# Converting 64-bit weight pieces in pairs, with stages at their own steps, in a fused attention and SwiGLU kernel

## The chip, the cores and the metric

The kernel runs on one core of a Trainium2 chip. A core has five engines with a queue of instructions each, which work side by side and wait for each other by semaphores: TensorE (PE) multiplies matrices, VectorE (DVE) and ScalarE (ACT) work element by element, GpSimd (POOL) does so too, and SyncE (SP) starts DMA transfers. Matrix results land in PSUM; all else is kept in SBUF, 128 partitions wide. The metric is the time of one execution on the device in microseconds (us), as the median of several. Each engine carries out its instructions in the order of the program, so an instruction that waits holds up all behind it on its engine.

## The reference

q, k and v have the shape (8 sequences, 12 heads, 448 tokens, 64), in float32. The output of attention is the input of a feed-forward block with 768 model columns and 1536 inner columns, whose weights are float64.

```python
def rmsnorm(x, g):
    rms = np.sqrt(np.mean(x * x, axis=-1, keepdims=True) + 1e-06)
    return x / rms * g
q_n, k_n = (rmsnorm(q, g_q), rmsnorm(k, g_k))
scores = 1.0 / np.sqrt(64) * np.matmul(q_n, k_n.transpose(0, 1, 3, 2))
attn = np.exp(scores - np.max(scores, axis=-1, keepdims=True))
attn = attn / (np.sum(attn, axis=-1, keepdims=True) + 1e-09)
x = np.matmul(attn, v)                    # then (8, 12, 448, 64) -> (3584, 768)
xn = x / np.sqrt(np.mean(x * x, axis=-1, keepdims=True) + 1e-06) * rms_g
g = xn @ w_gate                           # float64 weights
return ((g * (1.0 / (1.0 + np.exp(-g)))) * (xn @ w_val)) @ w_out
```

## The kernel before

**Blocks.** The work of attention is cut into 48 blocks `g`, each of two heads of one sequence; six blocks make a sequence. For each block TensorE turns q and k (`turn`, L544, L548), ScalarE and VectorE move them to SBUF (qT L549; kT L550, L552), TensorE makes the scores (`score` L562, `rests` L659), ScalarE the exponentials `e` (L566, L664), and one block later TensorE multiplies them with v (`values`, L576, L589, L674) and sums them over the keys (`den`, L580, L606, L692). VectorE inverts the sum and weighs the result into `x` (L596 to L598, L638). The norms of q and k are prepared two blocks ahead: ScalarE squares (L493), VectorE adds up (`ms`, L496), GpSimd raises to the power -1/2 (`rs`, L514, L515) and scales q (`qn`, L520); k is scaled by its norm within the exponential in the early blocks, and later by ScalarE beforehand (`norm_k`, L530). The last 64 tokens of the heads (`rest`) have steps of their own, on GpSimd L465, L466 and L469, in some blocks. GpSimd also adds the squares of `x` (`ss`, L644), for the norm of the rows (`rms_x`, L726 to L730; `norm_x`, L738, L744).

**Early and later blocks.** Blocks 0 to 6 have attention alone. From block 7 on the steps of attention stand between matrix products of the feed-forward block for the sequence before (L1440, L1081 and others), which are taken from a list `todo`. There the sums over keys are prepared by adding the six tiles of exponentials of a block into one (`later_sums`, `es`, L709 and L714), so that TensorE has fewer to add.

**The order of work.** It is written out in the program. Every step of TensorE goes through `pe(fn)`, which counts the step in `now["t"]` and then gives out what has fallen due; `after(n, fn)` sets work for n steps later. The order on each engine is that in which the program gives the instructions out.

**The weights.** [...] A weight is read as two 32-bit words, the low one and the high one, and put together to a float32 by integer operations. There are 72 pieces of 128 x 384 weights: 48 of gate and value, 24 of the output. A piece goes through this chain, in `convert`: SP loads both words into `raw` (384 KB); ScalarE makes `top` from the high words (Abs, L842) and scales the low words in place (L843), both at stride two, since the words alternate (`split`); VectorE limits `top`, shifts and masks it, and puts in the sign (`join`, L848, L849, L850); GpSimd adds low and top to the finished piece `w` (L890); SP stores a copy in DRAM (`keep`), because the pieces do not all fit in SBUF and are loaded again for each sequence. One call of `convert` takes one step of the chain for several pieces at once: the sum of piece n-5, the join of n-4, the split of n-3, the load of n, the copy of n-7. Early blocks call it three times each (`turns`, L1641 and L1644); later the list of products calls it before each product whose piece is not ready. `TURNS` is 79. Pieces wait in 7 buffers `raw`, 6 buffers `top` (and some of the pool `xs`), and 23 buffers `w`. When all are done, weights derived from sums and differences of pieces are made on VectorE (L1003) for later sequences, and the room of `raw` and `top` serves as further buffers.

The functions that the change touches, and what calls them, with the line numbers of the profile:

Of the kernel before, what the change touches and what calls it, by code (L numbers as in the profile page):

```python
# [25 lines left out]
BW = 384  # L26
# [309 lines left out]
def safe_scores(  # L336
# [367 lines left out]

    def later_sums(g, n):

        def first():
            st["es", g] = tmp.tile([128, S], F32, name="es", tag="es", bufs=2)
            nc.gpsimd.tensor_tensor(st["es", g], st["e", g, 0], st["e", g, 1], ALU.add)  # L709
            more(2)  # L710

        def more(*parts):
            for i in parts:
                nc.gpsimd.tensor_tensor(st["es", g], st["es", g], st["e", g, i], ALU.add)  # L714

        after(n, first)
        after(n + 2, lambda: more(3, 4))
        after(n + 3, lambda: more(5, 6))
# [97 lines left out]
    def room(n):  # L816
        return len(free_w) >= n
# [5 lines left out]
    def data(key):  # L823
        return st[key][0][:, 0:BW]

    def load_raw(src):
        raw = raw_pool.tile([128, 2 * BW], I32, name="raw")
        a = src.shape[1]
        nc.sync.dma_start(out=raw.rearrange("p (a n w) -> p a (n w)", a=a, w=2).bitcast(I64), in_=src)
        return raw  # L830

    def split(raw, n):


        words = raw.rearrange("p (n w) -> p n w", w=2)
        lo, hi = words[:, :, 0], words[:, :, 1]
        if n < 24 and n % 7 > 3:

            top = s_pool.tile([128, 3, HT], I32, name="xs")[:, 0:2].rearrange("p c n -> p (c n)")[:, 0:BW]
        else:  # L840
            top = cv_pool.tile([128, BW], I32, name="top")
        nc.scalar.activation(top.bitcast(F32), hi.bitcast(F32), ACT.Abs)  # L842
        nc.scalar.activation(lo, lo.bitcast(U32), ACT.Copy, scale=2.0**-29)  # L843
        return lo, hi, top

    def join(lo, hi, top):
# [4 lines left out]
        return lo, top  # L851


    pieces = []
# [10 lines left out]
    turn_of = {"n": 0}  # L865
    room_so = []
    TURNS = len(pieces) + 7

    def home(key):
        if key[0] == "w":  # L870
# [6 lines left out]
    def keep(key):  # L877
        nc.sync.dma_start(out=home(key), in_=data(key))

    def convert():  # L880

        n = turn_of["n"]
        if n >= TURNS or not room(1):
            return False
        turn_of["n"] += 1
        if 0 <= n - 5 < len(pieces):
            key = pieces[n - 5][0]
            st[key] = block()
            lo, top = st.pop(("cv", n - 5))
            nc.gpsimd.tensor_tensor(data(key).bitcast(I32), top, lo, ALU.add)  # L890
        if 0 <= n - 4 < len(pieces):
            st["cv", n - 4] = join(*st.pop(("cv", n - 4)))
        if 0 <= n - 3 < len(pieces):
            st["cv", n - 3] = split(st.pop(("raw", n - 3)), n - 3)
        if n < len(pieces):
            st["raw", n] = load_raw(pieces[n][1])
        if 0 <= n - 7 < len(pieces):
            keep(pieces[n - 7][0])
        if turn_of["n"] == TURNS:

            free_w.extend(cv_pool.tile([128, BW], F32, name="top") for _ in range(4))
            whole = [raw_pool.tile([128, 2 * BW], F32, name="raw") for _ in range(7)]
            room_so.extend(whole[:6])
            homes = [whole[6][:, 0:BW], whole[6][:, BW:]] + [cv_pool.tile([128, BW], F32, name="top")[:, :] for _ in range(2)]
            carried.extend(t.rearrange("p (c n) -> p c n", c=KG) for t in homes)
        return True

# [55 lines left out]

    def ask():

        if turn_of["n"] < TURNS:
            return
        while asked["n"] < len(uses):  # L970
            key = uses[asked["n"]]
# [483 lines left out]
    def gate_value_items(b):  # L1455

        if b == 0:
            return [(3 * S, 4 * (fc + 1) + 7, 0, fn) for fc in range(NFC) for fn in plain(fc)]
        return [(6 * HT, TURNS, 8 * (fp + 1) if b == 1 else 0, fn) for fp in range(NFP) for fn in quad(b, fp)]

    def out_items(b):
        if in_quads(b):
            return [(cost, TURNS, 0, fn) for cost, fn in out_quads(b)]
        if b >= FIRST_O:
            return [(NFP // 2 * HALF, TURNS, 0, fn) for fn in out_strassen(b)]
        tiles = out_pairs(b)[-1][1] + 1
        return [(NFC // OUT_PARTS * HALF, 4 * NFC + NFC * (n + 1) + 7, 0, lambda a=(b, n, i, part, i == tiles - 1): project_out(*a))
                for n in range(2) for i in range(tiles) for part in range(OUT_PARTS)]


# [3 lines left out]
    def fill(n=None):  # L1474
# [6 lines left out]
                part["spent"] += todo[n][0]  # L1481
                n += 1
        for _ in range(min(n, len(todo))):
            _, turns, sums_made, fn = todo.pop(0)
# [115 lines left out]
    for g in range(NG + 1):  # L1600
# [7 lines left out]
        if g == 0:  # L1608
# [6 lines left out]
            squares(2, 0)  # L1615
            squares(2, 1)
            pe(lambda: turn(1, 1))
            for _ in range(3):
                convert()
            load_pair(3)  # L1620
            load_v(2)
            convert()
            load_rows()
            continue
        if g <= NPAIR:
# [115 lines left out]
```

## Time and profile before

| what | us |
|---|---|
| median of 3 runs | 1545.07 (1543.91 to 1545.62) |
| the profiled execution | 1546.19 |
| its span, first to last instruction | 1544.4 |
| TensorE busy | 1511.2 (98%) |
| VectorE busy | 929.8 (60%) |
| GpSimd busy | 736.4 (48%) |
| ScalarE busy | 534.8 (35%) |
| mean granted TensorE clock | 0.996 |

The span is a little shorter than the time of the execution that it comes from. In the profile an instruction is named by engine, line, operation and tile (`w<-top,raw` reads top and raw and writes w), with its partitions x elements; `[2.93 <-ACT e L664]` behind it means that its engine stood idle 2.93 us before it, until the instruction on L664 of ScalarE had ended. In a row of waits stand the total, the count and the longest. In a row of windows stand, after the length, the busy time of PE, of its weight loads, of DVE, ACT and POOL with their instruction counts, then the granted clock, the share of the DMA engines and GB/s. Busy shares of the whole span mix stages: conversion fills the first 260 us, and the rest of the span has none of it.

### The profile page before, as it was taken

To read this page: it belongs to the slowest core of one execution; us is meant where nothing else is said; L and a number is where in the kernel's file an instruction comes from. 1 tells how busy PE (TensorE), PEld (TensorE's weight loads), DVE (VectorE), ACT (ScalarE), POOL (GpSimd) and SP (SyncE) were. 2 spreads that over 40 slices of the span, in tenths; PEclk is the share of its full clock that TensorE was granted. 3 is DMA by queue.
4 is the path that set the end of the run, shared out by engine and by line. 5 is a ranking of instruction groups with operands and counts; after the bars stand their busy time and mean duration, and the time that the engine had idled before them with its cause. 6 is when DMAs were issued, how large, how long until landed. Compare 5 with 4: busy or idle time off the path is not lost.

```text
span 1544.4 us, 26111 instructions
## 1 busy us (share of the span) xinstructions
PE 1511.2 (98%) x8900; PEld 1187.4 (77%) x8900; DVE 929.8 (60%) x1793; ACT 534.8 (35%) x1241; POOL 736.4 (48%) x718
## 2 busy tenths in 40 slices
PE   8999998999999999999999999999999999999997
PEld 4344444688856888888987888767987889899997
DVE  5788998667754666854457443444458444673464
ACT  6856664333323333234233332424333232101000
POOL 6868887546424354474435652544545731030003
PEclk9999999999999999999999999999999999999998
DMA  7758575776989978886557855584557755577565
GB/s 194 228 153 258 175 228 157 225 229 214 294 274 275 310 253 266 285 250 188 160 163 217 267 176 153 152 275 131 174 155 228 240 160 148 164 256 256 175 194 176
DMA packets 314082, 327.26 MB, mean 212 GB/s; under 512 B 84308, under 2 KB 310868, under 8 KB 313940
## 3 DMA queue, kind: packets, MB, share of 16 engines
q1 hardware_dynamic: 313012, 325.31, 68.1%
q8 instruction: 73, 1.20, 0.3%
q14 instruction: 69, 0.57, 0.1%
q10 hardware_dynamic: 800, 0.20, 0.1%
q0 software_dynamic: 128, 0.00, 0.0%
HBM read 271.62 MB, written 53.77 MB: 211 GB/s over the span
## 4 chain that ended last, share of the span: by engine, by line
PE 83%; DVE 11%; DMA 2%; issue 1%; ACT 1%; POOL 1%; SPq 0%; DVEq 0%; POOLq 0%; ACTq 0%
PE ff L1081 42%; PE ff L1373 10%; PE sc L659 7%; PE av L674 6%; PE ff L1305 5%; PE ff L1440 4%; PE tr L544 2%; PE ff L1178 2%; DVE top L850 1%; DVE top L849 1%; PE den L692 1%; PE den L606 1%; DVE top L848 1%; PE sc L562 1%; DVE l L1248 1%
## 5 line engine op out<-in xcount | busy, mean ns | idle before, releaser
L1081 PE MATMUL ff<-x,w 128*128 128x224 f32 x1686 | 344.4, 354 | 0.0
L1081 PEld LDWEIGHTS ff<-x,w 128*128 128x128 f32 x1686 | 315.2, 190 | 13.2 <-issue 11.3
L1081 PE MATMUL ff<-xs,w 128*128 128x224 f32 x1296 | 265.2, 353 | 2.0 <-DVE w L1003 1.2
L714 POOL TENSOR_TENSOR es<-es,e 128x448 f32<-128x448 f32 x205 | 245.9, 1200 | 13.7
L1081 PEld LDWEIGHTS ff<-xs,w 128*128 128x128 f32 x1296 | 243.9, 190 | 3.4 <-issue 1.5
L659 PE MATMUL sc<-qT,kT 64*64 64x448 f32 x1176 | 233.8, 542 | 5.7 <-ACT e L664 2.9
L674 PE MATMUL av<-e,vt 64*64 64x448 f32 x984 | 194.2, 541 | 0.0
L664 ACT ACTIVATE e<-sc 128x448 f32<-128x448 f32 x294 | 154.4, 547 | 71.4 <-PE sc L659 53.5
L644 POOL TENSOR_TENSOR ss<-ss,rd 128x448 f32<-128x448 f32 x40 | 48.0, 1201 | 218.5 <-ACT rd L643 218.5
L659 PEld LDWEIGHTS sc<-qT,kT 64*64 64x64 f32 x1176 | 79.3, 133 | 87.4 <-issue 61.6
L709 POOL TENSOR_TENSOR es<-e 128x448 f32<-128x448 f32 x41 | 48.2, 1176 | 178.0 <-ACT e L664 178.0
L515 POOL TENSOR_TENSOR rs<-ms,mhalf 128x12 f32<-128x12 f32 (+1 forms) x50 | 115.9, 2319 | 4.2
L1093 DVE TENSOR_TENSOR cc<-ff,u 128x448 f32<-128x448 f32 x84 | 52.3, 623 | 99.6 <-PE ff L1081 99.5
L1440 PE MATMUL ff<-x,w 128*128 128x448 f32 x288 | 111.8, 541 | 0.0
L674 PEld LDWEIGHTS av<-e,vt 64*64 64x64 f32 x984 | 66.2, 133 | 42.4 <-issue 42.4
L1100 ACT ACTIVATE th<-c 128x224 f32<-128x224 f32 x42 | 16.3, 389 | 238.1 <-DVE c L1093 238.1
L1373 PE MATMUL ff<-w,l 128*128 128x192 f32 x500 | 95.6, 329 | 2.8 <-DVE l L1248 2.0
L1440 PEld LDWEIGHTS ff<-x,w 128*128 128x128 f32 x288 | 53.3, 190 | 51.1 <-issue 49.2
L1373 PEld LDWEIGHTS ff<-w,l 128*128 128x128 f32 x500 | 82.6, 190 | 8.1 <-DVE l L1248 3.2
L1345 POOL TENSOR_TENSOR y<-y,c 128x384 f32<-128x384 f32 x10 | 12.2, 1217 | 159.4 <-DVE y L1414 148.0
L1093 DVE TENSOR_TENSOR u<-ff,p 128x448 f32<-128x448 f32 x42 | 26.2, 623 | 84.3 <-PE ff L1081 77.9
L1093 DVE TENSOR_TENSOR u<-ff,u 128x448 f32<-128x448 f32 x42 | 26.1, 623 | 82.6 <-PE ff L1081 82.3
(209 smaller groups left out, 2627.9 us busy)
## 6 DMA issues: line engine op xcount, KB each, us to landing
w<-kept SPq DMA_DIRECT2D x474, 192.0 KB, 3.7
w<-kept_q SPq DMA_DIRECT2D x297, 192.0 KB, 3.8
w<-kept_o SPq DMA_DIRECT2D x132, 192.0 KB, 3.9
kept<-w SPq DMA_DIRECT2D x81, 192.0 KB, 3.9
top<-kept SPq DMA_DIRECT2D x78, 192.0 KB, 3.9
top<-kept_q SPq DMA_DIRECT2D x53, 192.0 KB, 3.2
kept_q<-w SPq DMA_DIRECT2D x52, 192.0 KB, 3.0
qk<-in_q_dram SPq DMA_DIRECT2D x48, 192.0 KB, 3.5
```

The lines of the kernel that those rows point to most:

```text
L515: nc.gpsimd.tensor_tensor(st["rs", g][:, cols], ms, mhalf[:, cols], ALU.pow)
L644: after(m, lambda: (nc.gpsimd.tensor_tensor(ss, ss, rd, ALU.add), st.update({("summed", b): hp})))
L659: nc.tensor.matmul(ps[r, 0:S], lhsT=st["kT", g][r, keys_of(i)], rhs=st["qT", g][r, :], start=True, stop=True)
L664: nc.scalar.activation(e, ps[:, 0:S], ACT.Exp)
L674: nc.tensor.matmul(st["av", g][own(j), 0:S], lhsT=vt, rhs=st["e", g, i][r], start=i == 0, stop=i == PARTS - 1, skip_group_check=True)
L709: nc.gpsimd.tensor_tensor(st["es", g], st["e", g, 0], st["e", g, 1], ALU.add)
L714: nc.gpsimd.tensor_tensor(st["es", g], st["es", g], st["e", g, i], ALU.add)
L1081: nc.tensor.matmul(bank[:, w * HT:(w + 1) * HT], lhsT=wt[:, c * 128:(c + 1) * 128], rhs=x[:, c, :], start=onto is None and w == c == 0, st ...
L1093: nc.vector.tensor_tensor(add[name], ps[:, 0:S], add[other], ALU.add)
L1305: nc.tensor.matmul(ps, lhsT=left_o(b, which, LEFT_O[name], c), rhs=data(("wo", b, name, c)), start=first and c == 0, stop=c == NFP - 1, sk ...
L1373: nc.tensor.matmul(ps, lhsT=a[:, j, :], rhs=data(key)[:, n % 2 * HW:(n % 2 + 1) * HW], start=start and j == 0, stop=j == KG - 1, skip_grou ...
L1440: nc.tensor.matmul(bank[w][:, 0:S], lhsT=data(key)[:, c * 128:(c + 1) * 128], rhs=st["x", 0, half][:, c, :], start=half == c == 0, stop=ha ...
```

## The change

Pieces are now handled in pairs. `raw` holds two pieces, loaded by two transfers. `split` works on 768 elements at a time: it writes the scaled low words to a new buffer `low` without gaps, and writes the absolute high words in place of the low ones, at stride two within `raw`; the second instruction thus follows the first. `join` works on 768 elements at stride two within `raw`. The sum is still one instruction per piece, from `raw` at stride two and `low`. There are 4 buffers `raw` of two pieces, 3 buffers `low` of two pieces, 21 buffers `w`, and nothing is taken from `xs`.

`convert` no longer ties the stages together by a piece number. Each stage is given out when what it needs is at least two TensorE steps old: a copy after its sum, a join after its split, a split after its load. In the early blocks the joins and sums of two pairs are given out together before the sums of the block (`finish_pairs(2)`; in block 6 after the scores), and two splits and two loads after the scores (`begin_pairs(2)`); in block 5 this stands ahead of `norm_k`. The first two pairs are loaded in block 0, split in block 1, and joined and summed in block 2.

The sums of exponentials (`later_sums`) are made on VectorE while the copies of the pieces are not all given out, and on GpSimd after that.

```diff
-    NW = 23
+    NW = 21
-    raw_pool, cv_pool, l2_pool = pool("c_raw", 7), pool("c_cv", 6), pool("c_l2", 5)
+    raw_pool, cv_pool, l2_pool = pool("c_raw", 4), pool("c_cv", 3), pool("c_l2", 5)
...
     def later_sums(g, n):
+        engine = nc.vector if count["kept"] < ALL else nc.gpsimd
...
-            nc.gpsimd.tensor_tensor(st["es", g], st["e", g, 0], st["e", g, 1], ALU.add)
+            engine.tensor_tensor(st["es", g], st["e", g, 0], st["e", g, 1], ALU.add)
...
-                nc.gpsimd.tensor_tensor(st["es", g], st["es", g], st["e", g, i], ALU.add)
+                engine.tensor_tensor(st["es", g], st["es", g], st["e", g, i], ALU.add)
...
-    def split(raw, n):
+    def split(raw):
         words = raw.rearrange("p (n w) -> p n w", w=2)
         lo, hi = words[:, :, 0], words[:, :, 1]
-        if n < 24 and n % 7 > 3:
-            top = s_pool.tile([128, 3, HT], I32, name="xs")[:, 0:2].rearrange("p c n -> p (c n)")[:, 0:BW]
-        else:
-            top = cv_pool.tile([128, BW], I32, name="top")
-        nc.scalar.activation(top.bitcast(F32), hi.bitcast(F32), ACT.Abs)
-        nc.scalar.activation(lo, lo.bitcast(U32), ACT.Copy, scale=2.0**-29)
-        return lo, hi, top
+        low = cv_pool.tile([128, 2 * BW], I32, name="low")
+        nc.scalar.activation(low, lo.bitcast(U32), ACT.Copy, scale=2.0**-29)
+        nc.scalar.activation(lo.bitcast(F32), hi.bitcast(F32), ACT.Abs)
+        return lo, hi, low
...
+    def add_piece():
+        if not joined or not room(1):
+            return
+        (top, low), i = joined[0]
+        key = pieces[len(added)][0]
+        st[key] = block()
+        cols = slice(i * BW, (i + 1) * BW)
+        nc.gpsimd.tensor_tensor(data(key).bitcast(I32), top[:, cols], low[:, cols], ALU.add)
+        joined.pop(0)
+        added.append(now["t"])
+    def join_pair():
+        if halved:
+            both = join(*halved.pop(0)[0])
+            joined.extend((both, i) for i in range(2))
+    def split_pair():
+        if loaded and len(halved) + (len(joined) + 1) // 2 < 3:
+            halved.append((split(loaded.pop(0)[0]), now["t"]))
+    def load_raws():
+        n = count["loaded"]
+        if n < ALL and n - len(added) < 7:
+            loaded.append((load_raw([src for _, src in pieces[n:n + 2]]), now["t"]))
+            count["loaded"] += 2
     def convert():
...
+        old = lambda jobs, n: jobs and jobs[0][1] <= now["t"] - n
+        if count["kept"] < len(added) and added[count["kept"]] <= now["t"] - 2:
+            keep(pieces[count["kept"]][0])
+            count["kept"] += 1
+        if len(added) % 2 == 0 or not added or added[-1] < now["t"]:
+            load_raws()
+        add_piece()
+        if len(joined) < 2 and old(halved, 2):
+            join_pair()
+        if old(loaded, 2):
+            split_pair()
...
-            while turn_of["n"] < turns:
-                if not convert():
-                    pe(idle)
+            while len(added) < ready:
+                convert()
+                pe(idle)
...
-    def turns(n):
+    def finish_pairs(n):
         for _ in range(n):
-            convert()
+            join_pair()
+            add_piece()
+            add_piece()
+        while count["kept"] < len(added) and added[count["kept"]] < now["t"] - 2:
+            keep(pieces[count["kept"]][0])
+            count["kept"] += 1
+    def begin_pairs(n):
+        for _ in range(min(n, len(loaded))):
+            split_pair()
+        for _ in range(n):
+            load_raws()
...
-            turns(1 if g == 1 else 3 if g < NPAIR else 0)
+            if g < NPAIR:
+                finish_pairs(2)
             pe(lambda: sums(g - 1))
             pe(lambda: score(g, (1, 2)))
-            turns(2 if g == 1 else 3 if g == NPAIR else 0)
+            if g == NPAIR:
+                finish_pairs(2)
+            begin_pairs(2)
             if g == 2:
                 bound()
             if g == NPAIR - 1:
                 for half in range(2):
                     norm_k(g + 2, half)
             continue
```

More of the change, by code (lines that the diff above doesn't have):

```diff
@@ L824, in data, with load_raw, join @@
         return st[key][0][:, 0:BW]
[L826 to L829, printed above, removed]
+    def load_raw(srcs):
+        raw = raw_pool.tile([128, 4 * BW], I32, name="raw")
+        for i, src in enumerate(srcs):
+            part = raw[:, i * 2 * BW:(i + 1) * 2 * BW].rearrange("p (a n w) -> p a (n w)", a=src.shape[1], w=2)
+            nc.sync.dma_start(out=part.bitcast(I64), in_=src)
         return raw
-    def split(raw, n):
+    def split(raw):
         words = raw.rearrange("p (n w) -> p n w", w=2)
         lo, hi = words[:, :, 0], words[:, :, 1]
-        if n < 24 and n % 7 > 3:
-            top = s_pool.tile([128, 3, HT], I32, name="xs")[:, 0:2].rearrange("p c n -> p (c n)")[:, 0:BW]
-        else:
-            top = cv_pool.tile([128, BW], I32, name="top")
-        nc.scalar.activation(top.bitcast(F32), hi.bitcast(F32), ACT.Abs)
-        nc.scalar.activation(lo, lo.bitcast(U32), ACT.Copy, scale=2.0**-29)
-        return lo, hi, top
-    def join(lo, hi, top):
+        low = cv_pool.tile([128, 2 * BW], I32, name="low")
+        nc.scalar.activation(low, lo.bitcast(U32), ACT.Copy, scale=2.0**-29)
+        nc.scalar.activation(lo.bitcast(F32), hi.bitcast(F32), ACT.Abs)
+        return lo, hi, low
+    def join(top, hi, low):
         nc.vector.tensor_scalar(top.bitcast(F32), top.bitcast(F32), 122879.9921875, 2.0**-15, ALU.min, ALU.max)
@@ L850, in join @@
         nc.vector.scalar_tensor_tensor(top, hi, -(2**30), top, ALU.bitwise_and, ALU.bitwise_or)
-        return lo, top
+        return top, low
     pieces = []
@@ L864, in safe_scores @@
             pieces.append((("wo", 0, *block_of(n, fc)), cols.rearrange("p (a n) -> p a n", a=1)))
-    turn_of = {"n": 0}
+    loaded, halved, joined, added = [], [], [], []
+    count = {"loaded": 0, "kept": 0}
     room_so = []
-    TURNS = len(pieces) + 7
+    ALL = len(pieces)
     def home(key):
@@ L878, in keep @@
         nc.sync.dma_start(out=home(key), in_=data(key))
-    def convert():
[L882 to L904, printed above, removed]
+    def add_piece():
[8 more added lines that the diff above has]
+        added.append(now["t"])
@@ new lines, in convert @@
+    def convert():
+        if count["kept"] == ALL:
+            return
+        old = lambda jobs, n: jobs and jobs[0][1] <= now["t"] - n
[9 more added lines that the diff above has]
+            split_pair()
+        if count["kept"] == ALL:
+            ends = [cv_pool.tile([128, 2 * BW], F32, name="low") for _ in range(3)]
+            free_w.extend(t[:, i * BW:(i + 1) * BW] for t in ends for i in range(2))
+            whole = [raw_pool.tile([128, 4 * BW], F32, name="raw") for _ in range(4)]
+            room_so.extend(whole[i // 2][:, i % 2 * 2 * BW:(i % 2 + 1) * 2 * BW] for i in range(6))
+            homes = [whole[3][:, i * BW:(i + 1) * BW] for i in range(4)]
@@ L905, in convert @@
             carried.extend(t.rearrange("p (c n) -> p c n", c=KG) for t in homes)
-        return True
     def out_pairs(b):
@@ L966, in ask @@
     def ask():
-        if turn_of["n"] < TURNS:
+        if count["kept"] < ALL:
             return
@@ L1457, in gate_value_items @@
         if b == 0:
-            return [(3 * S, 4 * (fc + 1) + 7, 0, fn) for fc in range(NFC) for fn in plain(fc)]
-        return [(6 * HT, TURNS, 8 * (fp + 1) if b == 1 else 0, fn) for fp in range(NFP) for fn in quad(b, fp)]
+            return [(3 * S, 4 * fc + i + 1, 0, fn) for fc in range(NFC) for i, fn in enumerate(plain(fc))]
+        return [(6 * HT, ALL, 8 * (fp + 1) if b == 1 else 0, fn) for fp in range(NFP) for fn in quad(b, fp)]
     def out_items(b):
         if in_quads(b):
-            return [(cost, TURNS, 0, fn) for cost, fn in out_quads(b)]
+            return [(cost, ALL, 0, fn) for cost, fn in out_quads(b)]
         if b >= FIRST_O:
-            return [(NFP // 2 * HALF, TURNS, 0, fn) for fn in out_strassen(b)]
+            return [(NFP // 2 * HALF, ALL, 0, fn) for fn in out_strassen(b)]
         tiles = out_pairs(b)[-1][1] + 1
-        return [(NFC // OUT_PARTS * HALF, 4 * NFC + NFC * (n + 1) + 7, 0, lambda a=(b, n, i, part, i == tiles - 1): project_out(*a))
+        return [(NFC // OUT_PARTS * HALF, 4 * NFC + NFC * (n + 1), 0, lambda a=(b, n, i, part, i == tiles - 1): project_out(*a))
                 for n in range(2) for i in range(tiles) for part in range(OUT_PARTS)]
@@ L1483, in fill @@
         for _ in range(min(n, len(todo))):
-            _, turns, sums_made, fn = todo.pop(0)
-            while turn_of["n"] < turns:
-                if not convert():
-                    pe(idle)
+            _, ready, sums_made, fn = todo.pop(0)
+            while len(added) < ready:
+                convert()
+                pe(idle)
             while asked["derived"] < sums_made:
@@ L1617, in safe_scores @@
             pe(lambda: turn(1, 1))
-            for _ in range(3):
-                convert()
+            load_raws()
             load_pair(3)
             load_v(2)
-            convert()
+            load_raws()
             load_rows()
```

## The prediction

> **What bounds the kernel now.** I read the page's busy table first, then TensorE's waits over the first 300 us, then the time windows, and last the single instructions around the places this led to.
>
> ```profile
> PE 1511.2 (98%) x8900; PEld 1187.4 (77%) x8900; DVE 929.8 (60%) x1793; ACT 534.8 (35%) x1241; POOL 736.4 (48%) x718
> ```
>
> TensorE is busy for 98% of the span, so all that another engine can give back is its idle time. The waits show where that lies while weights are converted (the first 300 us):
>
> ```profile
> PE tr L544 <- DVE kT L550: 3.2, 1, 3.2
> PE sc L659 <- ACT e L664: 2.9, 1, 2.9
> PE sc L659 <- DVE x L744: 2.7, 1, 2.7
> PE rb L738 <- POOL rs L730: 0.7, 1, 0.7
> PE msx L726 <- POOL ss L644: 0.7, 1, 0.7
> ```
>
> The windows say which engine is full (busy time of PE, PEld, DVE, ACT, POOL, then the granted clock):
>
> ```profile
> 25.00:95.00 70.00, 68.27 (x361) 26.70 (x361) 53.95 (x113) 52.42 (x111) 57.02 (x59) 1.00 0.70 208
> 95.00:165.00 70.00, 70.00 (x292) 33.98 (x289) 64.00 (x105) 44.24 (x102) 55.31 (x51) 1.00 0.64 200
> 165.00:200.00 35.00, 32.07 (x168) 14.73 (x170) 33.19 (x48) 19.90 (x45) 29.62 (x29) 1.00 0.56 173
> 200.00:232.00 32.00, 32.00 (x153) 15.12 (x146) 29.28 (x44) 21.96 (x50) 25.58 (x25) 1.00 0.81 261
> 232.00:262.00 30.00, 24.09 (x109) 13.02 (x111) 29.35 (x45) 12.95 (x31) 23.07 (x22) 1.00 0.59 177
> 262.00:300.00 38.00, 38.00 (x190) 21.46 (x183) 21.57 (x34) 14.36 (x33) 18.49 (x19) 0.96 0.55 173
> ```
>
> From 95 to 262 VectorE is busy for 155.8 of 167 us, GpSimd for 133.6. The three large waits hang on that pair; in the first of them ScalarE's next split had stood 6.03 us for a GpSimd sum to free its buffer:
>
> ```profile
> 197.88 0.55 ACT L842 ACTIVATE top<-raw 128x384 f32<-128x384 f32 x1 [6.03 <-POOL w L890]
> ```
>
> After the third wait the clock falls to 0.96 over the window: the five pairs of score and value steps from 262.29 to 266.01 take 3.72 us, where five at the 0.375 of the trace around 200 us take 1.87, which costs 1.85 us. So the conversion stretch holds 2.93 + 3.17 + 2.74 + 1.85 = 10.7 us that a lighter VectorE and GpSimd could return.
>
> The early blocks (20 to 90 us) are another matter: TensorE waits for nothing there, at a period of 10.45 us a block, but GpSimd is already full. One early block with rests reads so (start, length, instruction):
>
> ```profile
> 55.82 1.14 POOL L644 TENSOR_TENSOR ss<-ss,rd 128x448 f32<-128x448 f32 x1 [0.22 <-ACT rd L643]
> 57.05 0.25 POOL L514 TENSOR_SCALAR ms<-ms 128x12 f32<-128x12 f32 x1
> 57.38 2.43 POOL L515 TENSOR_TENSOR rs<-ms,mhalf 128x12 f32<-128x12 f32 x1
> 59.89 1.22 POOL L520 TENSOR_TENSOR qn<-qk,rs 128x192 f32<-128x192 f32 x2
> 61.20 0.44 POOL L465 TENSOR_SCALAR msr<-msr 128x6 f32<-128x6 f32 x1
> 61.72 1.35 POOL L466 TENSOR_TENSOR msr<-msr,mhalf 128x6 f32<-128x6 f32 x1
> 63.15 0.83 POOL L469 TENSOR_TENSOR rest<-rest,msr 128x384 f32<-128x384 f32 x1
> 63.94 2.98 POOL L890 TENSOR_TENSOR w<-top,raw 128x384 int32<-128x384 int32 x3
> ```
>
> The sums of the pieces come last in the block, behind the norm of the next q and k.
>
> **The change part by part.**
>
> *Pairs.* Before, a piece costs VectorE 148.2 us / 70 = 2.12 us (L848, L849, L850 from 25 to 262 us). Undisturbed the three start 0.385, 0.395 and 0.475 us apart, 1.26 together, so 0.86 per piece (0.29 per instruction) is waiting beside GpSimd. A pair of 768 elements: the first two process 384 in 0.35 us, two a cycle by their slope against L850's 0.56, so they grow by 0.2 us to 0.585 and 0.595, the third by 0.4 to 0.875: 2.05 free. New is that the one-input pair runs in place at stride two, which no row shows on VectorE. Lower bound: no price (L850 reads its high words at stride two and takes 0.56, L1003 of the same size without it 0.55). Upper bound: one element a cycle, as L850 runs, 0.875 each, 2.63 a pair. I take the lower, nearest in kind. The Trainium skill, "VectorE: DVE Perf Modes", section "What auto-detection actually checks", says that a single-source operation in SBUF gets two elements a cycle by even outer dimensions, with no word of the step for 32-bit data. The row of 0.35 us for 384 agrees, and by the rule the pair would cost the same 2.05; no row shows it at stride two.
>
> *Sums of exponentials on VectorE.* 7 blocks (7 to 13) x 6 = 42 sums leave GpSimd (42 x 1.2 = 50 us) for VectorE. The nearest row is the two-input L1003, 0.54 start to start. With GpSimd's data work down from about 105 us (50 of sums, 55 of pieces) to 55, I halve the waiting to 0.14 per instruction: 0.68 each, 28.6 us; bounds 0.54 (22.7) and 0.83 (34.9, waiting unchanged). The skill has a rule against this: "SBUF — State Buffer", section "SBUF: two separate sides", says that a VectorE operation with two SBUF inputs and a GpSimd one that reads SBUF lock each other out for the whole instruction. The 0.86 us of waiting per piece above agrees with it in kind. Were each of the 42 to wait half of a 1.0 us GpSimd sum, they would cost 42 x 1.04 = 44 us; by that VectorE would be nearly as full as now, and with half of the gain lost the forecast would be 1557.
>
> *VectorE from 95 to 262.* About 52 pieces remain there, 26 pairs. 155.8 - 52 x 2.12 + 26 x (2.05 + 0.43) + 28.6 = 138.7 of 167 us, 83% where it was 93%; with both upper bounds (2.63 + 0.86 a pair, 34.9) it is 171, over full. GpSimd falls to about 84. So the waits on VectorE and GpSimd should go, -10.7. What is late next: ScalarE's split waits for one of three pair buffers, so two new waits of about 1 us (one GpSimd sum, 1.0) come back: +2.1. Net -8.6; bounds -10.7 and 0.
>
> *ScalarE.* One split of a pair is two instructions of 768, the second waiting for the first: by the rows 128x384 0.56 and 0.455 start to start against 64 elements at 0.257, about 0.85 each, 1.7 together (before: 4 x 0.455 = 1.82). No cost by itself; ScalarE is 63% busy from 95 to 165 us.
>
> *Fewer buffers, and the early blocks.* This is where I see the loss. Before, three pieces a block were split beside the work. Now the second pair of each early block takes the slot of the pair three before, and this is freed by the second of the first two piece sums of the same block. Behind that split on ScalarE stand the next block's exponentials e(0), its squares, qT and rd; behind these GpSimd's ss, ms, rs and qn; behind these, rests and piece sums. That closes a loop: in the trace before, e(0) starts at 52.85 and the first sum behind it at 63.94, 11.1 us; two sums 2.0; the split 1.7; together 14.8 us with rests (blocks 3 and 4), 12.1 without (2.7 less), against TensorE's 10.45. Unrolled: block 1's two pair splits before e(0) move block 3 by +1.55 (values of block 2 at 44.85, before 43.30), and w1 ends at 44.1. Then e(0) of block 3 at 45.8, its qn at 54.2 and w5 at 59.0; e(0) of block 4 at 60.7, its qn 69.1, w9 73.8; e(0) of block 5 at 75.5, its qn 83.9, w13 85.9. TensorE's values step follows qn by 0.95: block 4 at 55.3 (53.76 before, hidden behind the +1.55), block 5 at 70.05 (64.21). In block 5 the scaling of k (six L530, 1.54) is now behind the waiting split: 85.9 + 1.7 + 1.5 = 89.1, and 0.4 of transposes: 89.5 where it was 75.52, +14.0. Bounds: the loop is put together from single rows, and if one GpSimd operation of it (1.2) is hidden in each of four turns, +9; if GpSimd loses 0.5 a turn more beside the longer joins, +16.
>
> *Block 6.* Two joins and four sums now stand before the row norm (L728, L730 before): a second split ends at about 15.0 us after the values step, the score that takes its slot wanted 14.6 to 15.2: +1.0 (bounds 0 and 2). *The clock.* Three stalls of some 4.4 us follow (block 5; then qn and L530 in block 6). The row at 262 shows 1.85 lost after one of 2.74; the first two are covered by the next stall, the last is not: +1.9 (bounds 0 and 3.8). *SP.* Raw loads go two at a time and wait for GpSimd's sums of the pair four before; 4.4 us to land against a block's lead: nothing, and if the cover goes, the splits would wait behind the same loop. *Conversion ends* three steps later, and the first derived weights (L1003) are wanted right before their use: 0 to 0.5, taken as 0.
>
> **Sum.** 14.0 + 1.0 + 1.9 - 8.6 = +8.3, against the profiled execution's 1546.19 us (its span 1544.4): 1554.5. That execution lies 1.12 over the median of 1545.07, so 1553.4 on the median's scale; I say 1553.
>
> **The rivals.** 0.2% is 3.1 us, about what can be told from no change: faster is under 1542.0, slower over 1548.2.
>
> *A, faster:* the early loop is mostly slack. With no clock loss it decides where the early loss stays under 4.5 (8.6 - 1.0 - 3.1). That needs each of four turns of the loop to be 2.4 us shorter ((14.0 - 4.5) / 4), by GpSimd being ahead when the split asks. For it: before, GpSimd stood idle 2.91 us at 78 us. Against it: from 44.4 to 66.9 it stands less than 1 us in all. An early loss of 1 to 3, block 6's 1.0 and a gain of 10.7 to 9 give 1536 to 1540.
>
> *B, more slower:* the middle gain does not come, because VectorE takes one element a cycle at stride two, and with the sums is as full as before. Then 1545.07 + 16.9 = 1562. For it: no row of the kind; against it: L850 and the contiguous row agree.
>
> *C, no difference:* early loss 9 (the lower bound above), block 6's 1.0, no clock loss, gain 8.6: 1546.5.
>
> **How the numbers follow.** Forecast 0.57, A 0.16, B 0.14, C 0.13. The forecast's own range is 1548.5 to 1558 (early loss 11 to 15, block 6 and clock together 2 to 4, gain 10 to 6: +3 to +13). The range leaves out most of A and the upper half of B: 1541 to 1562. Slower: 0.57 + 0.14 = 0.71; the same 0.13; faster 0.16.
>
> **What would show it.** Right: TensorE idle from about 60 to 90 us, released by GpSimd qn and ScalarE's scaling of k, ScalarE waiting there for GpSimd sums of pieces; the waits at 199, 240 and 261 us gone; VectorE near 83% in the middle. Wrong: the early blocks still at 10.45 us a block; L847 and L848 of the change well over 0.65 us undisturbed; new TensorE waits on sums (es) or x in the middle.

## The result and the profile after

The changed kernel takes 1594.45 us (median, 1592.77 to 1595.13) against 1544.34 before in the same session: a ratio of 1.0324, with a 95% interval from 1.031 to 1.0337. It is slower by 50 us, where 8 were forecast. The sign was right; the time lies far outside the range that was given, and outside the slower rival too.

Two points of TensorE's program stand in both traces and divide the loss: the values step of block 1 (L576), and the groups of sums over keys (L692), the first for block 7, then one for every two blocks. The time from the values step of block 1 to the first group is called the early stretch here, the time from the first to the fourth group the middle.

| | before | after | difference |
|---|---|---|---|
| values step, block 1 | 18.95 | 19.09 | 0.1 |
| values step, block 4 | 53.76 | 58.28 | 4.5 |
| values step, block 5 | 64.21 | 74.00 | 9.8 |
| values step, block 6 | 75.52 | 93.31 | 17.8 |
| first group of L692 | 116.14 | 136.90 | 20.8 |
| second group | 168.00 | 202.83 | 34.8 |
| third group | 220.77 | 268.56 | 47.8 |
| fourth group | 287.61 | 336.12 | 48.5 |
| early stretch | 97.2 | 117.8 | +20.6 |
| middle | 171.5 | 199.2 | +27.7 |

After that the two run alike (the fifth groups, at 342.31 and 390.87, are 48.6 apart). So 21 us are lost early, and the middle, from which a gain of 8.6 was forecast, loses 28.

The engines' shares and the windows of the changed kernel (same columns as before):

```profile
PE 1528.9 (96%) x8900; PEld 1191.9 (75%) x8900; DVE 908.3 (57%) x1727; ACT 532.9 (33%) x1169; POOL 700.8 (44%) x676
...
25.00:95.00 70.00, 56.73 (x265) 22.70 (x267) 36.65 (x70) 47.33 (x83) 48.60 (x48) 0.91 0.61 187
95.00:165.00 70.00, 61.90 (x266) 26.60 (x261) 49.44 (x75) 33.38 (x62) 32.69 (x28) 0.94 0.55 166
165.00:200.00 35.00, 31.27 (x128) 14.70 (x127) 23.12 (x33) 15.79 (x29) 18.66 (x18) 0.95 0.48 153
200.00:232.00 32.00, 26.21 (x116) 11.82 (x115) 22.47 (x32) 17.62 (x32) 18.10 (x16) 0.89 0.52 167
```

VectorE does less than before in all, as the change means it to, and yet TensorE is idle in every window; no engine is full. From 95 to 232 us VectorE is busy for 95.0 of 137 us (126.5 before), GpSimd for 69.5 (110.5 before), in part because less of the work is reached by then. Where every engine has room and TensorE still waits, the order of the work is the first suspect. TensorE's waits in the first 400 us:

```profile
PE sc L659 <- ACT rd L699: 10.1, 2, 5.8
PE tr L544 <- POOL qn L520: 9.3, 4, 3.1
PE sc L659 <- ACT e L664: 9.2, 3, 4.8
PE sc L659 <- ACT rd L696: 5.6, 1, 5.6
PE tr L544 <- ACT qk L530: 3.2, 1, 3.2
```

The second and the fifth row are the early blocks, by the releasers that were forecast (GpSimd's qn, ScalarE's scaling of k). The other three hold five stalls of 3.7 to 5.8 us, one in each of five blocks of the middle (and one wait of 0.7 us before it); all wait for ScalarE, which is busy for 66.8 of 137 us there, about half of the time. What ScalarE stands for is in its own instructions, here the second split of blocks 2 to 5:

```profile
45.31 0.91 ACT L841 ACTIVATE low<-raw 128x768 int32<-128x768 uint32 x1 [1.98 <-POOL w L888]
60.99 0.93 ACT L841 ACTIVATE low<-raw 128x768 int32<-128x768 uint32 x1 [4.40 <-POOL w L888]
76.71 0.94 ACT L841 ACTIVATE low<-raw 128x768 int32<-128x768 uint32 x1 [5.82 <-POOL w L888]
89.57 0.91 ACT L841 ACTIVATE low<-raw 128x768 int32<-128x768 uint32 x1 [3.25 <-POOL w L888]
```

and for the first stall of the middle in the chain that ended last (start, length, engine, tile and line; "SPq" is SyncE's queue):

```profile
134.77 0.54 POOL qn L520
...
135.58 0.51 POOL qn L520
136.09 2.60 POOL w L888 x2
138.68 0.02 issue
138.70 0.38 SPq L832
139.08 0.04 issue
139.13 4.22 DMA raw<-in_moe_w_val_dram
...
143.45 0.91 ACT low L841
144.36 0.02 issue
144.38 0.90 ACT raw L842
145.28 0.41 ACT rd L696
145.70 0.04 issue
145.74 1.01 PE sc L659 x2
```

Read forward: GpSimd finishes the norm of q and only then comes to its piece sums, which the program gave out behind it. Two sums free a buffer `raw`; SyncE, which stood waiting for that, starts the next load, and it lands 4.22 us later; ScalarE, which stood waiting for that, splits; behind the split stand the copy of a sum over keys (`rd`) and the exponentials, and TensorE waits for those. Another split, at 138.71, had stood 5.67 us for the same sums. Each of the engines' instructions is short. The chain is long because each stage is the next thing in the queue of an engine that has other work behind it.

### The profile page after: what moved, and what is told of

It is laid out like the page before. It is cut to its first block, busy times and chain, and to the rows that moved or that the text cites. A ratio compares the mean times of both kernels' runs of the same rounds, so it can differ in the third digit from the quotient of the medians.

```text
span 1592.4 us, 25888 instructions
## 1 busy us (share of the span) xinstructions
PE 1528.9 (96%) x8900; PEld 1191.9 (75%) x8900; DVE 908.3 (57%) x1727; ACT 532.9 (33%) x1169; POOL 700.8 (44%) x676
## 4 chain that ended last, share of the span: by engine, by line
PE 78%; DVE 7%; POOL 5%; DMA 3%; ACT 3%; issue 3%; SPq 1%; POOLq 0%; ACTq 0%; DVEq 0%
PE ff L1105 42%; PE ff L1397 11%; PE sc L659 8%; PE av L674 6%; PE ff L1329 5%; POOL w L888 2%; PE ff L1202 1%; POOL rs L515 1%; PE tr L544 1%; DMA raw<-in_moe_w_out_dram 1%; DVE l L1272 1%; PE den L692 1%; PE ff L1464 1%; DMA raw<-in_moe_w_val_dram 1%; DVE ms L496 1%
## 5 line engine op out<-in xcount | busy, mean ns | idle before, releaser
L1105 PE MATMUL ff<-x,w 128*128 128x224 f32 x1560 | 321.8, 354 | 0.0
L1105 PEld LDWEIGHTS ff<-x,w 128*128 128x128 f32 x1560 | 291.3, 190 | 14.6 <-issue 13.4
L659 PE MATMUL sc<-qT,kT 64*64 64x448 f32 x1176 | 246.2, 564 | 25.0 <-ACT rd L699 10.1
L1105 PE MATMUL ff<-xs,w 128*128 128x224 f32 x1188 | 244.4, 353 | 2.2 <-DVE w L1027 1.2
L1105 PEld LDWEIGHTS ff<-xs,w 128*128 128x128 f32 x1188 | 223.4, 190 | 4.3 <-issue 2.2
L716 POOL TENSOR_TENSOR es<-es,e 128x448 f32<-128x448 f32 x170 | 203.1, 1195 | 11.7
L888 POOL TENSOR_TENSOR w<-raw,low 128x384 int32<-128x384 int32 x72 | 83.1, 1178 | 36.1 <-PE ff L1464 14.1
L1105 PE MATMUL ff<-x,low 128*128 128x224 f32 x456 | 97.2, 353 | 0.0
L1464 PEld LDWEIGHTS ff<-x,w 128*128 128x128 f32 x288 | 53.8, 192 | 53.0 <-issue 51.2
L1105 PEld LDWEIGHTS ff<-x,low 128*128 128x128 f32 x456 | 85.5, 190 | 2.1 <-issue 1.4
L514 POOL TENSOR_SCALAR ms<-ms 128x12 f32<-128x12 f32 (+1 forms) x50 | 16.0, 319 | 156.3 <-DVE ms L496 155.0
```

Source lines behind the costliest of these rows:

```text
L659: nc.tensor.matmul(ps[r, 0:S], lhsT=st["kT", g][r, keys_of(i)], rhs=st["qT", g][r, :], start=True, stop=True)
L716: engine.tensor_tensor(st["es", g], st["es", g], st["e", g, i], ALU.add)
L888: nc.gpsimd.tensor_tensor(data(key).bitcast(I32), top[:, cols], low[:, cols], ALU.add)
L1105: nc.tensor.matmul(bank[:, w * HT:(w + 1) * HT], lhsT=wt[:, c * 128:(c + 1) * 128], rhs=x[:, c, :], start=onto is None and w == c == 0, st ...
L1464: nc.tensor.matmul(bank[w][:, 0:S], lhsT=data(key)[:, c * 128:(c + 1) * 128], rhs=st["x", 0, half][:, c, :], start=half == c == 0, stop=ha ...
```

## The experiments

The early stretch loses 21 us and the middle 28; this may have one cause or two. Theory 1: a split on ScalarE waits for a buffer `low` that GpSimd's sums free late. Theory 2: the sums of exponentials on VectorE are at fault. Theory 3: the loads start too late and their landing is what counts. All times are medians, "before" was timed along with each.

| run | edit | time | ratio to before, 95% interval | early | middle |
|---|---|---|---|---|---|
| before | | 1544.3 | | 97.2 | 171.5 |
| after | | 1594.5 | 1.0324 (1.031 to 1.0337) | 117.8 | 199.2 |
| e1 | after, es on GpSimd | 1602.9 | 1.0384 (1.0366 to 1.0401) | 117.7 | 204.4 |
| e2 | after, 4 buffers low | 1590.9 | 1.0299 (1.0282 to 1.0316) | 111.8 | 202.5 |
| e3 | after, early order | 1577.5 | 1.0216 (1.0199 to 1.0233) | 101.2 | 198.2 |
| e4 | before, es on VectorE | 1543.7 | 0.9995 (0.9985 to 1.0004) | 97.2 | 169.8 |
| e5 | e3, distance of 2 steps | 1565.2 | 1.0131 (1.0114 to 1.0148) | 101.0 | 187.9 |
| e6 | e3, distance of 4 steps | 1549.8 | 1.0032 (1.002 to 1.0043) | 101.1 | 171.5 |
| e7 | e3, single pieces | 1573.2 | 1.0192 (1.0165 to 1.0218) | 105.1 | 192.8 |
| e8 | e7, distance of 2 steps | 1560.6 | 1.0105 (1.0086 to 1.0124) | 105.2 | 178.9 |
| e9 | after, distance of 4, early join | 1562.4 | 1.0113 (1.0097 to 1.0129) | 117.5 | 168.0 |
| e10 | e3 and e9 together | 1545.4 | 1.0006 (0.9998 to 1.0015) | 101.1 | 165.6 |
| e11 | e10, es on GpSimd | 1555.2 | 1.0066 (1.0051 to 1.0082) | 101.1 | 176.8 |
| e12 | e10, one pair in blocks 3 and 4 | 1548.6 | 1.0025 (1.0015 to 1.0034) | 99.7 | 171.2 |

**e1: the sums of exponentials back on GpSimd.**

```diff
-        engine = nc.vector if count["kept"] < ALL else nc.gpsimd
+        engine = nc.gpsimd
```

> The changed kernel with the sums of exponentials back on GpSimd throughout. Theory 1 (the split on ScalarE waits for a low buffer that GpSimd's piece sums free late, behind the norm of q): GpSimd gets 42 x 1.2 = 50 us more in the conversion stretch, its piece sums come later, and the time rises from 1594 to 1600-1615; the early blocks stay as they are (values step of block 6 at 93 us). Theory 2 (the sums of exponentials on VectorE delay the joins and with them everything): the time falls by 15 us or more, to under 1580.

1602.9 us, the early stretch unchanged, the middle 5 us longer. Theory 2 falls: within this change the move to VectorE helps.

**e2: a fourth buffer low.** Two buffers `w` make room for it, and the limit on split pairs goes from three to four. Conversion ends four TensorE steps later by this (counted in the programs).

```diff
-    NW = 21
+    NW = 19
-    ... pool("c_cv", 3) ...
+    ... pool("c_cv", 4) ...
```

> The changed kernel with four pair buffers low in place of three, and 19 buffers w in place of 21, so that a split waits for the sums of the pair four before. Theory 1: the early blocks lose the loop, the values step of block 6 comes at 76-80 us where it is 93.3 (75.5 before the change), and in the middle the waits of 5 to 7 us of ScalarE's split for GpSimd's sum go, TensorE's five stalls shrink to the 3 us that the landing of raw adds: 1560-1570. Theory 3 (the loads are the cause: a load starts only when a sum has freed raw, and the split two steps later waits for its landing): the middle stays within 8 us of what it is, 1572-1580.

1590.9 us: neither theory's number. The early stretch gains 6 us and no more, although no split waits for a sum there now; the middle gains nothing. ScalarE's waits from 30 to 330 us have changed their partner:

```profile
ACT low L841 <- DMA raw<-in_moe_w_gate_dram: 30.5, 5, 10.2
ACT low L841 <- DMA raw<-in_moe_w_out_dram: 28.6, 5, 8.5
ACT th L1472 <- PE ff L1464: 21.1, 10, 4.0
```

Where the buffer `low` no longer holds the split, the load does, which waits for `raw` from the same sums: two buffers with one releaser. And early, the waiting was only part of it: the two splits (4 x 0.92 us) still stand ahead of the block's last exponentials, of the squares and of qT, and so ahead of the norm on GpSimd that TensorE needs next. That this place is the rest of the early loss is a reading here; e3 tests it.

**e3: the splits ahead of the joins, in the early blocks.** The pairs that are split in a block are joined and summed in it. On ScalarE the splits now come behind the block's first exponentials, squares and qT. In block 1 nothing is split any more.

```diff
-            if g < NPAIR:
+            if g > 1:
+                begin_pairs(2)
+            if 1 < g < NPAIR:
                 finish_pairs(2)
             pe(lambda: sums(g - 1))
             pe(lambda: score(g, (1, 2)))
             if g == NPAIR:
                 finish_pairs(2)
-            begin_pairs(2)
+                begin_pairs(2)
```

> The changed kernel, only the early blocks reordered: from block 2 on the two splits and loads stand ahead of the joins and sums of the same block, so that a split needs no sum of its own block. Theory 1: the values step of block 6 falls from 93.3 to 76-80 us and the time by 13 to 18 us, to 1577-1581; the middle stays. Rival (the early loss comes of longer splits and joins, not of the slot): block 6 still after 85 us, the time over 1586.

1577.5 us, within the number of Theory 1: 17 us come back from the new order alone. The values step of block 6 stands at 76.80. The early stretch is 101.2 us long: of the 20.6 us that it had lost, e2, which took away the waits alone, gave back 6.0, and e3, which takes away the waits and the place of the splits, gives back 16.6. TensorE's waits from the start to 330 us show that only the middle is left:

```profile
PE sc L659 <- ACT rd L699: 10.4, 2, 5.9
PE sc L659 <- ACT e L664: 8.5, 2, 4.8
PE sc L659 <- ACT rd L696: 6.2, 1, 6.2
```

**e4: the sums of exponentials on VectorE, in the kernel before.**

```diff
+        engine = nc.vector if turn_of["n"] < TURNS else nc.gpsimd
-            nc.gpsimd.tensor_tensor(st["es", g], ...)
+            engine.tensor_tensor(st["es", g], ...)
```

> The kernel before, only with the sums of exponentials on VectorE until all pieces are converted. Theory 2: VectorE, 93% busy from 95 to 262 us, gets 42 x 0.7 to 0.83 = 29 to 35 us more than GpSimd's relief returns: slower by 5 to 20 us. Rival (GpSimd's relief is worth more, since VectorE waits 0.86 us a piece beside it and the wait at 199 us is GpSimd's): faster by 2 to 8 us.

No difference, and so neither number: 1543.7 us against 1543.9 before. The middle is 1.7 us shorter in the one trace. By itself this part of the change neither costs nor gains.

**The distance.** The order in which the programs give out work has a quantity that no row of a profile shows: how many TensorE steps lie between the sum that frees a buffer and the split that takes it. Counted in the programs for the later blocks:

| | split after its freeing sum | split after its own load |
|---|---|---|
| before | 5 to 9 steps | 4 to 8 |
| after, e3 | 0 to 2 (now and then 5) | 2 to 3 (now and then 5 or 6) |
| e2 | 3 to 8 | 2 to 3 (now and then 5 or 6) |
| e5 | 2 to 3 (now and then 5 or 6) | 3 to 8 |
| e6 | 4 to 8 | 5 to 10 |
| e10 | 4 to 7 | 5 to 9 |

A step of the feed-forward is six matrix multiplications, some 2.3 us. GpSimd is behind by up to a norm (4.5 us) and several sums. With 0 to 2 steps the split is on ScalarE before its buffer can be free. In e2 the first column is repaired and the second is not. From e5 on both columns grow at once, so these runs do not say how much of the middle is due to each.

**e5 and e6: a minimum distance.** A split is given out only if the sum that frees its buffer was given out 2 (e5) or 4 (e6) steps before.

```diff
+        freed = lambda i, n: i < 0 or (i < len(added) and added[i] <= now["t"] - n)
+        pairs_split = count["loaded"] // 2 - len(loaded)
-        if old(loaded, 2):
+        if old(loaded, 2) and freed(2 * (pairs_split - 3) + 1, 4):
```

The last line is that of e6; in e5 it ends in 2.

> The reordered early blocks, and later a split is given out only two TensorE steps or more after the sum that frees its low buffer (now 0 to 2 steps, before the change 5 to 9). Theory 1 (the split stands on ScalarE for a sum that GpSimd reaches late, and the exponentials behind it stop TensorE): TensorE's stalls of 4 to 6 us in each block of the middle shrink to under 2, the time falls from 1577 to 1550-1560. Rival (VectorE or the landing of raw limits the middle): 1570 or more.

1565.2 us: better by 12 us, but not by as much as expected. Two steps are too few: ScalarE still waits 34.8 us for sums from 90 to 330 us, and three of TensorE's stalls are left, of 4.5 to 7.0 us.

> As the run with two steps, with four steps between the freeing sum and the split; conversion ends six TensorE steps later. Theory 1: ScalarE waits for no piece sum any more, the middle is as fast as before the change or faster: 1543-1552. Rival (pieces come too late then and TensorE waits for them, or VectorE is the limit): 1565 or more.

1549.8 us, within the range, and the middle is at its length of before (171.5). The sign that went with it did not come: ScalarE still waits for piece sums, 26.8 us in seven waits from 90 to 330 us (16.7 us in six before the change), but it waits much less for loads (3.6 us, where 15.8 in e3), and none of TensorE's stalls is over 2 us. TensorE's waits from 60 to 330 us now begin with the products of the output projection, which wait for late pieces:

```profile
PE ff L1204 <- POOL w L888: 4.5, 5, 1.9
PE sc L659 <- ACT e L664: 1.4, 1, 1.4
```

This goes with the six steps by which conversion ends later.

**e7 and e8: pieces instead of pairs.** Here the stages keep their own steps, but each works on one piece (8 buffers `raw`, 6 `low`, of one piece each). The diff shows two of the edits. e8 also asks for three steps between a load and its split, in place of two, and for two between the freeing sum and the split.

```diff
-    raw_pool, cv_pool, ... = pool("c_raw", 4), pool("c_cv", 3), ...
+    raw_pool, cv_pool, ... = pool("c_raw", 8), pool("c_cv", 6), ...
-        low = cv_pool.tile([128, 2 * BW], I32, name="low")
+        low = cv_pool.tile([128, BW], I32, name="low")
```

> The reordered early blocks, and single pieces in place of pairs (8 buffers raw, 6 low, of one piece each; each instruction on 384 elements), at the same own steps. The split still comes 1 or 2 steps after the sum that frees its buffer. Theory 1: the middle stays as bad, and pays 36 x 0.5 us more of fixed time on VectorE besides: 1574-1590. Rival (the pairing itself, whose second half holds both buffers and doubles the length of each instruction): 1560 or less.

1573.2 us, just under the number of Theory 1. It is 4 us faster than with pairs: the early stretch is 4 us longer, the middle 5 us shorter. So most of the loss of the middle is not due to pairing; 21 us of it stay without it.

> As the run with single pieces, a split two to six steps after the freeing sum and three after its load. Theory 1: 1548-1560, as with the pairs. Rival (pairing is what costs or gains): more than 8 us from the run with pairs and two steps, to either side.

1560.6 us, 4.6 under the pairs with two steps, within the 8 us allowed and above the range for the time. The longer distances are worth 13 us for pieces, where those of e5 were worth 12 for pairs.

**e9 and e10: a distance of four steps that delays nothing.** The join is given out one step after the split rather than two. This frees the buffers a step sooner, and conversion ends at the same step as in the changed kernel.

```diff
-        if len(joined) < 2 and old(halved, 2):
+        if len(joined) < 2 and old(halved, 1):
             join_pair()
-        if old(loaded, 2):
+        if old(loaded, 2) and freed(2 * (pairs_split - 3) + 1, 4):
```

> The changed kernel with its own early blocks; later a split comes four steps or more after the sum that frees its buffer, and the join one step after the split instead of two, so that conversion ends at the same step. Theory 1 (two separate losses: the split ahead of the next block's exponentials early, the short distance to the freeing sum later): the early 18 to 20 us stay (values step of block 6 at 93), the middle's 28 go: 1562-1568. Rival (the middle is slow because it starts late): 1575 or more.

1562.4 us: the early stretch loses its 20 us as in the changed kernel, and the middle falls to 168.0 from 199.2. The two losses are separate. The edit has two halves, the distance and the earlier join; the earlier join was not run without the distance.

> Both edits: the splits ahead of the joins in the early blocks, and the distance of four steps with conversion ending at the same step. Theory 1: no stall over 2 us in the middle, and no wait for late pieces at the end of it (4.5 us in the run with six late steps): 1540-1546, as before the change or a little faster. Rival (VectorE or GpSimd full in the middle): 1550 or more.

1545.4 us against 1544.7 before, a ratio of 1.0006 (0.9998 to 1.0015): no difference. With two edits, neither of which changes an instruction, the 50 us are gone. The five stalls are too; TensorE's waits from 25 to 330 us:

```profile
PE tr L544 <- DVE kT L550: 2.2, 1, 2.2
PE sc L659 <- ACT e L664: 1.6, 1, 1.6
PE msx L728 <- POOL ss L644: 1.2, 1, 1.2
PE tr L544 <- POOL qn L520: 1.2, 1, 1.2
```

and the windows show what the pairs and the move to VectorE do once the stalls are gone:

```profile
95.00:165.00 70.00, 70.00 (x302) 34.27 (x299) 59.16 (x87) 39.52 (x76) 36.55 (x32) 1.00 0.70 214
165.00:200.00 35.00, 34.74 (x166) 16.25 (x169) 28.77 (x42) 19.68 (x36) 25.79 (x25) 1.00 0.49 152
200.00:232.00 32.00, 30.23 (x156) 13.74 (x149) 24.74 (x35) 22.11 (x40) 17.86 (x17) 1.00 0.77 245
232.00:262.00 30.00, 27.75 (x122) 14.93 (x124) 28.31 (x40) 15.54 (x27) 18.11 (x16) 1.00 0.51 167
```

VectorE is busy for 141.0 of 167 us (155.8 before), GpSimd for 98.3 (133.6), and the middle is 5.9 us shorter than before. The early stretch is 3.9 us longer, and most of the gain is spent there; both figures are of one execution each, and the medians show no gain.

The waits of ScalarE are not gone. Its waits for piece sums from 25 to 350 us are these, in the kernel before, the changed kernel and e10:

```profile
ACT top L842 <- POOL w L890: 16.7, 6, 6.0
ACT low L841 <- POOL w L888: 57.3, 12, 7.4
ACT low L841 <- POOL w L888: 24.9, 7, 7.1
```

In e10 only the longest of the seven stops TensorE for more than 0.3 us, by 1.6 (the second row of TensorE's waits above). In the changed kernel each of the five stalls had two such waits in a row ahead of it: 3.7 to 7.3 us for the sums, and behind that split 2.7 to 3.3 us for the landing of the next pair.

**e11: e10 with the sums of exponentials on GpSimd** (the edit of e1).

> As the run with both edits, with the sums of exponentials back on GpSimd throughout. If the move to VectorE is worth something once the splits no longer wait: 3 to 10 us slower than that run (GpSimd has 50 us more in the middle, its piece sums free the buffers later). If it is worth nothing, as it was in the kernel before: within 2 us.

1555.2 us, 9.8 over e10. Next to pairs with three buffers the move to VectorE is worth 10 us; next to the old chain (e4) nothing.

**e12: one pair in blocks 3 and 4**, where GpSimd has the rests as well.

```diff
-                begin_pairs(2)
+                begin_pairs(1 if g in (3, 4) else 2)
-                finish_pairs(2)
+                finish_pairs(1 if g in (3, 4) else 2)
```

> As the run with both edits, but one pair instead of two in blocks 3 and 4, where GpSimd has the rests too; conversion then ends four steps later. If GpSimd's four sums in those blocks cause what is left of the early loss (2.5 us to the values step of block 6), this goes: values step of block 6 at the distance of before (56.6 us after that of block 1); the late end costs 0 to 5 us: 1538-1546.

1548.6 us, above the range. The early stretch gains 1.5 us, and the distance from block 1 to block 6 is 57.7 us (59.1 in e10, 56.6 before). So the load on GpSimd in those two blocks is behind about half of the 2.5 us that are left there. The later end of conversion seems to cost more (middle 171.2 against 165.6): the difference lies between the third and the fourth group, where TensorE waits 2.1 us for late pieces and its granted clock is 0.97, not 1.00. No version here beats the kernel before. The early stretch is still 2.5 us longer than before, and where these lie was not tried; in e10 block 6 still shows a wait for GpSimd's ss (1.2 us), as the changed kernel does.

## Why the prediction was right and wrong

**Early blocks: the loop is there, short in size, and not the only path.** The loop was forecast from the program: the second split waits for the sums of its own block, and ScalarE's next block waits behind it. The trace has it, with waits of 1.98, 4.40, 5.82 and 3.25 us. The step of the forecast that is off is the length of a turn. Forecast values steps were 55.3, 70.05 and 89.5 for blocks 4, 5 and 6; they came at 58.28, 74.00 and 93.31. From one waiting split to the next (45.31, 60.99, 76.71) a turn takes 15.7 us, where 14.8 was forecast: the split took 1.87 (1.7 assumed), GpSimd's power 2.63 (2.4) and its qn 1.97 (1.3), and the first turn starts 1.2 later than reckoned. The bound of +16 was passed by 1.8. Block 6 and the clock were put at 2.9 together; from block 6 to the first group the difference grows by 3.0. e2 and e3 add something that the prediction did not see: most of the loss comes without the wait, too. e2 removed every such wait, and 14.6 of the 20.6 us stayed; e3, with the splits in another place as well, left 4.0. With the splits ahead of the next block's norm a turn is longer than TensorE's block even when no split waits.

**Middle: wrong, and by the largest term.** The failing step is "what is late next": the prediction saw that a split waits for one of three pair buffers and put this at two waits of about 1 us, +2.1. ScalarE waited 57.3 us for such sums from 25 to 350 us, 39 of them after the early blocks, and 18.2 us more for loads; TensorE stalled five times there, 24.2 us in all. In place of a gain of 8.6 us the middle lost 27.7. The error was to price a wait by the length of the instruction waited for (one sum, 1.0 us). It has to be priced by how far that instruction's engine is behind: the sums stood behind a norm, and that behind a wait for VectorE's ms. The early loop had been worked out in just this way; the same three buffers in the middle were not. The second failing step is SyncE's: loads were costed at nothing for 4.4 us "against a block's lead". In the middle the split follows mostly 2 to 3 steps behind a load that is itself held up, and the chain above shows the landing in full. How the 27.7 us divide between the two buffers stays open. Of the signs that were named, the early ones came; the waits at 199, 240 and 261 us went, but five longer ones took their place; and VectorE was busy for 69% from 95 to 232 us, not near 83%.

**The clock.** One stall of the early stretch was charged with 1.9 us; none of the middle was, as no stall was expected. After the first of the five the pairs of score and value steps start some 0.75 us apart:

```profile
145.74 1.01 PE L659 MATMUL sc<-qT,kT 64*64 64x448 f32 x2 [5.62 <-ACT rd L696]
146.54 0.96 PE L659 MATMUL sc<-qT,kT 64*64 64x448 f32 x2
147.29 0.96 PE L659 MATMUL sc<-qT,kT 64*64 64x448 f32 x2
```

Seven of them take from 145.74 to 151.02, 5.28 us, where seven at 0.375 take 2.62: 2.7 lost. After the last it is 275.32 to 280.60, the same. Over the five stalls some 12 us go this way, an estimate by the same count. With the 24.2 that is 36 us, against the 38 that the middle lost (27.7, and the 10.7 us of old stalls that it no longer has).

**VectorE's price: right for the stride, low for the waiting.** 138.7 us (83%) were forecast from 95 to 262 us; e10, without the stalls, has 141.0 (84%). The open price was the pair at stride two, in place (the changed kernel):

```profile
120.15 0.55 DVE L847 TENSOR_SCALAR raw<-raw 128x768 f32<-128x768 f32 x1
120.74 0.56 DVE L848 TENSOR_SCALAR raw<-raw 128x768 int32<-128x768 int32 x1
121.34 0.96 DVE L849 SCALAR_TENSOR_TENSOR raw<-raw 128x768 int32<-128x768 int32 x1
122.21 0.62 DVE L711 TENSOR_TENSOR es<-e 128x448 f32<-128x448 f32 x1
```

From 384 elements before to 768 now, the first two grow by some 0.20 us (from 0.35) and the third by 0.40 (from 0.56), so the first two run at twice its rate: the lower bound was right. The rule of the Trainium skill ("VectorE: DVE Perf Modes", "What auto-detection actually checks") names even or equal outer dimensions for a single source in SBUF, and no step. The rows agree with it. Rival B, more slower because of this price, was wrong in its cause, though its time of 1562 was the nearest.

The waiting was put too low: with it a pair took 2.72 us on average in e10, where 2.48 was forecast, 6 us more over 26 pairs. That the total is only 2.3 us off is partly luck, as the rest of VectorE's work in that stretch came out smaller. The sums of exponentials took 0.70 us on average (L716) in the changed kernel and 0.77 in e10, where 0.68 was forecast. The rule of "SBUF — State Buffer" ("SBUF: two separate sides") speaks of a lock for the whole instruction. The prediction's estimate beside it, half a GpSimd sum each, was 1.04. The measured times are well below that: in the changed kernel 20 of the 42 sums had no GpSimd operation beside them and took 0.62, the other 22 took 0.82.

**The gain of the middle: right in direction, once the stalls are gone.** 8.6 us were forecast, and e10's trace shows 5.9. Rival A (the early loop is slack) and C are refuted by the early rows.

## What to carry to other kernels

Before a chain of stages is re-timed, count for every buffer how many steps lie between the instruction that frees it and the one that takes it, and set that against how late the freeing engine runs, not against how long the freeing instruction takes. A stage that may wait belongs behind, and not ahead of, what the bounding engine needs next from the same queue. Two buffers that are freed by the same instruction have to be given their distance together: repairing one only moved the wait to the other (e2). Then look at the bounding engine's own waits: what another engine waits counts only where it reaches that engine (e10 keeps 24.9 us of ScalarE's waits, and TensorE stands some 2 us for ScalarE).

## What was not expected of the hardware

TensorE's matrix steps ran at half their rate after each stall of 3.7 to 5.8 us in the middle of the changed kernel, for some 3 to 5 us (granted 0.58 from 146 to 152 us), so that a stall of 5 us cost about 7.5. Shorter gaps are less certain: in the kernel before, one of 2.74 us was followed by half rate, but after one of 2.93 us the pairs kept starting 0.375 us apart. On VectorE an in-place operation with one input at stride two over 32-bit words took 0.55 us for 768 elements, against 0.35 for 384 contiguous ones before; no row here has 768 contiguous ones. On ScalarE a 768-element operation took 0.92 us at stride two, while two of 384 had started 0.455 apart, so that pairing saved ScalarE nothing. The same move of 42 sums from GpSimd to VectorE was worth 0 us in one order of work (e4) and 10 us in another (e11).
